# States' products by column halves, a softmax in token halves, and a new order of all steps, in an attention and SoLU feed-forward kernel

## The chip, the cores and the metric

The kernel runs on one core of one Trainium2 chip. The metric is the device time of one execution in microseconds. PE is the tensor engine, DVE the vector engine, ACT the scalar engine, POOL the engine GpSimd, SP the engine that issues the transfers.

## The reference: what is computed

Eight batch entries b with eight heads each hold 512 tokens x and 32 states. Tokens read the states, and states read the tokens, each with a softmax; the results, concatenated by heads, are 4608 rows of 512 (per entry 512 tokens and 32 states). Each row goes through a feed-forward layer with a softmax-gated activation and a layer norm.

```python
scores = scale * np.matmul(x, state.transpose(0, 1, 3, 2));  a = softmax(scores)   # +1e-9 in the sum
xread = np.matmul(a, state)
scores2 = scale * np.matmul(state, x.transpose(0, 1, 3, 2)); a2 = softmax(scores2)
sread = np.matmul(a2, x)
x = concat([xread, sread], axis=2)            # as 4608 rows of 512
h = x @ w_in                                  # 512 -> 1024
solu = h * softmax(h)
ln = (solu - mean(solu)) / np.sqrt(var(solu) + 1e-06) * g_ln
out = ln @ w_out                              # 1024 -> 512
```

The host lays the inputs out; w_in and w_out arrive as 64-bit words, of which the kernel makes float32.

## The kernel before

For a token, `xread @ w_in` equals `a @ (state @ w_in)`, summed over heads. So the kernel first makes, for each entry, the product of its states with w_in (step V, a matrix of 256 x 1024, in two blocks j of 128 rows), and H is then the attention weights times that matrix. State reads go the direct way, through w_in itself.

All work is written as small generators, one per step, each with `yield` between its instructions. The names of steps, as they stand in ORDER and in the prediction:

- `l n`: load of a block of w_in (n = 0 to 7: four row chunks c, left and right half of the columns; even n are the left halves) or of w_out (n = 8 to 15). `cl n`, `c n`: making float32 of it, a rounding on ACT (tile r) and three steps on DVE or POOL (tile wf). `wi c`, `wg f`, `wo n`: splits of w_in into a high and a low part (whi, wlo), scaling of w_out by g (wog), and its split (wohi, wolo).
- `Ls`, `G`: load of the states and their copies (s2). `LT`, `Ln`: loads of x, transposed and plain. `Lg`: four small loads of g.
- `V b i`: products of the states of entry b with column half i of w_in, and their copies out of PSUM (tiles swps, then vt or swf). `Y`, `Z`: V of entries 2 to 7 goes to memory and comes back later. `P`: its split into high and low part (swh, swl).
- `S b`: scores. `E b`: softmax over tokens, for the states' reads, and a bounce through memory (e2T, e2b). `A b`: softmax over states, for the tokens (a, m, z, aT), and its split (ath, atl). `R b`: reads of the states (srps).
- `H t`, t = 0 to 33: the 128 x 1024 tile h of token tile t. `C t`: its chain, a maximum (sm), an exponential (e), a product (u), centring, squares, and the inverse root. `D t`: transpose of u on DVE (ub), out to memory (ut) and back in another layout (back). `T t`: its split into uh and ul. `O t`: output products, the scaling (osb), and the store.
- `K`: one product of the identity with itself into a bank that nobody reads, a warming product.

Entry 0 uses the float32 matrices as they are (two products per half of an H step), the other entries and output tiles from 2 on use three products of high and low parts.

PSUM is split into two tiles h of two banks each (pool ps_h) and four single banks (pool ps_t), which scores, V, R and O share. SBUF's large blocks come from one pool of 45 slots; the column of per-tile numbers, sm, has four slots.

The order is written out by hand: the string ORDER names the step that is to go on next, and each token issues the instructions up to the next `yield` (`K*48` is 48 of them). Every engine runs its own instructions in this order and waits where an operand isn't ready, so one that waits holds up everything behind it on its engine. A second table, OPT, says for each step which engine takes it (a for ACT, d for DVE, p for POOL). All transfers are issued by SP, in order, and each waits until the eighth one before it has landed.

Of the kernel before, what the change touches and what calls it, by code (L numbers as in the profile page):

```python
# [28 lines left out]
OPT = dict(ph=2, k4=45, direct=[0, 1], hn=[0], on=[0, 1], s2='dpad', add='dpppdpdpdppppppp', whi='aada',  # L29
           wlo='ddpp', wg='aaaaaada', woh='aaaa', wol='dddd', ev='aaaaaaaadaaaaaaaaaadaaadaaaadddd',  # L30
           swh='aaaaaddadadadaaa', swl='ppdpddpppdddddpp', sub='dddpppdd', mul='ppddpdpp', ath='aaaaadda',
           alo='ddddddpp', up='aaaaaaaaadddaddadaddaadaadaaaaddda',
           uh='aaaaaddaaaddaaaaaaddddaadddddddaaaaaddaaaadddaadadaddaaadaaaddaaaaad',
           ul='ppppdppppppppdppddppppdddppppppdddddppddppppdddpdppppppddpdppdpdddpp',
           oe='aaaaaddaaddddadaadadadaddaaddddaaa')
# [3 lines left out]
E0 A0 c1 LT21 cl3 A0 E0 wi0 E0 l5 l6 G2 Lg A0 E0 cl4 A0 Ln01 G2 A0 c2 Ln10 c2 c3 c2 A0 K*48 S1 Ln11 A0 l7 c4 A0 c4  # L39
l8 cl5 l9 c5*2 A0 l10 c5 c4 E0 cl6 c3 l11 c6 c3 c6 l12 wi1 c6 l13 E1 A1 E1*2 l14 c7*2 cl7 K*50 V00 E1 l15 cl8 c7 c8  # L40
V00*2 Ln20 E1 c8 E1 K*6 V01 c8 LT30 cl9 E1*2 wg0 V01 c9*2 V01 K*7 H0 E1 A1 cl10 c9 A1 V10 cl11 LT31 A1 wg1 R0 Ln21
V10 R0 c10*2 V10 H0 R0 cl12 Ln30 c10 c11 A1 V11 Ln31 c12 wg2 c12 R0 wo4 C0 H1 c12 V11 R0*2 A1 V11 V20 C0 A1 H1 V20
A1 P10 C0 E1 V20 V21 C1 C0 H2 c13 V21 D0 V21 Y20 V30 C0 Y21 c14*2 D0 H2 c13 V30 C0 c11 V30 A1 P11 V31 c11 C1 C2 V40
wo4 V31 V40 R1 Y30 C1 V40 R1 P11 V31 V41 R1 C1 P10 Y31 V50 V41 H3 V50 Y40 V41 D0 V50 c15 Y41 C1 c15 V51 Z20 wi0 C2
C1 V60 D1 H3 V51 V60 Y50 V51 D1 V60 C2 V61 Y51 A1 C3 V70 V61*2 Y60 H4 A1 H4 T0 Y61 V71 T0 V70 P20 V70 H4 O0 V71 C2
V71 O0 Y70 wi1 D1 C2 O0 Y71 Z21 D2 H4 wg3 Z30 C2 H4*2 C3 wi2 D2 O0 R1 wg4 C3 wi2 S2 cl13 R1*2 O0 cl14 Z31 E2 C3 A2
H5 c14 H5 A2 H5 C3 A2 H5 c13 H5 T1 H5 A2 T1 O1 C3 cl15 O1 wo5 D3 E2 O1 c15 E2 wo5 O1 D3 A2 O1 D2 wg5 wg6 E2 wg7 O0
A2 E2 wi3 O0 A2 D3 O0 E2 A2 wi3 O1 wo6 E2 O1 O0 O1 T2 O0 C4 wo7 O2*2 T2 O2 O1 T2 O2 T3 T2 C4 C5 O2 O1 O3*2 wo7 C5
T3 O3*2 O2 C4 O2*2 C5 H6 C4 H6*2 T3 D4 H6 C5 H6 T3 H6 D4 O3 C5 O3 D5 O3*2 C4 C5 wo6 H7 D5 H7*2 C4 P21 O3 P21 O3*3
D4 O2 O3 O2 D5 O2 C6 O2 H7 O2 H7 Z40 P20 Z41 H7 T4 O2 S3 LT40 E2 C6 T4 O4 E3 E2 O4 T4 T5 O4 E3 C6 E3 T5 O5*3 E3 C6  # L50
T4 O5 T5 O5 C6 O5 O3 O4 E3 D6 T5 O5 E3 O5 C7 O5 D6 C6 O5*2 E3 E2 C7 O5 E3 O4*2 O5 E3 O4*2 A2 D6 O4*2 C7 A2 O4*2 P30
R2 C7 A2 R2 LT41 O4 E3 H8*2 R2 D7 C7 O4 R2 H8*2 R2 C7 R2 D7 A3 H8 T6 H8 A3 H9 T6 A3 H9 S4 C8 T6 A3 H9*2 E4 C8 H9 T6
# [20 lines left out]
H25*2 T22 O20 C24 O22 A7 O22*2 O20 C24 O22 A7 O20 O22*2 C25 C24 H26*2 A7 H26 C24 O21 H26*2 D24 H26 T23 C24 O22 C25
O23 A7 D24 O23 T23 A7 O23 T23 O23*3 O22*2 C25 T23 O23*2 C25 O23*2 D25 O23 C25 D24 O23 H27 O23 D25 C25 H27 P71 E7
H27*2 T24 P70 H27 A7 E7 O24*2 T24 O24 D25 A7 O24 H27 P71 O22 T24 O24 E7 O24 O22*2 R6 O22 A7 C26 R6 T25 O22 O24 O25
C27 C26 O25*2 R6 O25 T24 C27 C26 R7 O23 R7 C27 T25 C26 H28*2 C26 H28 D26 H28*2 C27 T25 C26 H28 D26 H29*2 C27 D27
T25 H29*3 D27 C27 H29 D26 O25*5 D27 O25*3 O24 O25 O24*2 C28 O24*2 T26 R6 C28 O24 T26 O26*2 R7 O24 C29 R7 T27 O26
# [552 lines left out]
```

## Time and profile before

| what | us |
|---|---|
| median of 3 runs | 384.27 (383.28 to 384.5) |
| profiled execution, device time | 384.67 |
| its span | 382.6 |
| PE busy | 370.2, of it 34.5 warming products |
| DVE busy | 316.1 |
| ACT busy | 204.8 |
| POOL busy | 170.0 |
| mean granted clock of PE | 0.997 |

Busy times are of the profiled execution. A row of the timeline gives the start in us from the span's start, the duration, engine, line, operation, output and inputs, and a count of instructions; in square brackets stand the idle time ahead of it and who ended that. A row of groups gives the busy time in us and the mean of one in ns, then idle time ahead and its causes. A row of stages gives, for each stretch, the busy time of each engine, the granted clock of PE, the busy share of the DMA engines and GB/s. Fp32 products leave two records each. Matmuls overlap, so the time of one on PE is read from the starts of those that follow.

### The profile page before, as it was taken

Reading aid. Unit: us, or ns where it says so; the run is one execution under the profiler, and the core shown is the slowest. Engines: PE = TensorE matmul, PEld = TensorE weight load, DVE = VectorE, ACT = ScalarE, POOL = GpSimd, SP = SyncE. Lnnn points to the kernel's source line nnn. Section 1 sums busy time; section 2 is a strip of 40 time slices with the busy share of each in tenths; the row PEclk is TensorE's granted clock in tenths of the full one; section 3 lists DMA queues with packets and bytes.
Section 4 is the critical chain, followed back from the end, with each engine's and each line's share of the span. In section 5 each row is a group of like instructions: output and inputs, shape, how many; then the busy total and the mean of one; then the engine's idle time right before and its main releaser. Section 6 shows DMA issues by size and latency. Waiting matters only on the chain.

```text
span 382.6 us, 6649 instructions
## 1 busy us (share of the span) xinstructions
PE 370.2 (97%) x2482; PEld 275.5 (72%) x2482; DVE 316.1 (83%) x421; ACT 204.8 (54%) x328; POOL 170.0 (44%) x229
## 2 busy tenths in 40 slices
PE   8999998999999999998999999999999999999994
PEld 8878433354677688775678887886878787888884
DVE  0899999979979999998998899898999928748420
ACT  1525797979656684526325266672673639234510
POOL 1144245157466345864245423645517835324220
PEclk9999999999999999999999999999999999999998
DMA  7999995997179928869966649359644662444431
GB/s 260 338 395 396 403 354 232 356 400 272 61 229 338 349 90 284 334 188 276 373 242 210 204 151 316 138 189 339 230 146 178 209 220 114 161 164 137 167 138 55
DMA packets 47051, 92.18 MB, mean 241 GB/s; under 512 B 4140, under 2 KB 25900, under 8 KB 47020
## 3 DMA queue, kind: packets, MB, share of 16 engines
q1 hardware_dynamic: 47020, 91.77, 68.0%
q8 instruction: 19, 0.31, 0.3%
q14 instruction: 12, 0.10, 0.1%
HBM read 54.53 MB, written 37.22 MB: 240 GB/s over the span
## 4 chain that ended last, share of the span: by engine, by line
PE 41%; DVE 29%; DMA 20%; issue 4%; ACT 3%; SPq 1%; POOL 0%; DVEq 0%; ACTq 0%; POOLq 0%
PE o L525 24%; PE h L451 14%; DVE ub L488 3%; DVE sm L458 3%; DVE u L464 3%; DMA st<-stB_dram 3%; DMA raw<-w_out_dram 3%; DMA back<-ut 3%; DVE ul L134 3%; DMA raw<-w_in_dram 3%; DMA xn<-xn_dram 2%; DMA ut<-ub 2%; DMA kept<-vt 2%; DMA xT<-xT_dram 2%; DVE uh L131 1%
## 5 line engine op out<-in xcount | busy, mean ns | idle before, releaser
L134 POOL TENSOR_TENSOR ul<-back,uh 128x512 fp32r<-128x512 f32 x39 | 52.1, 1341 | 50.1 <-DVE uh L131 26.8
L525 PE MATMUL o<-wohi,uh 128*128 128x512 f32 (+1 forms) x264 | 70.3, 388 | 1.2 <-DVE osb L534 0.9
L525 PE MATMUL o<-wolo,uh 128*128 128x512 f32 (+1 forms) x264 | 70.0, 385 | 0.0
L525 PE MATMUL o<-wohi,ul 128*128 128x512 f32 (+1 forms) x264 | 69.1, 384 | 0.4 <-DVE ul L134 0.4
L461 ACT ACTIVATE e<-h,sm 128x1024 f32<-128x1024 f32 x34 | 37.9, 1116 | 52.8 <-DVE sm L458 47.8
L525 PEld LDWEIGHTS o<-wohi,uh 128*128 128x128 f32 x264 | 48.2, 188 | 13.4 <-issue 3.1
L525 PEld LDWEIGHTS o<-wohi,ul 128*128 128x128 f32 x264 | 48.6, 188 | 11.4 <-DVE ul L134 1.1
L525 PEld LDWEIGHTS o<-wolo,uh 128*128 128x128 f32 x264 | 48.5, 188 | 9.8
L458 DVE TENSOR_REDUCE sm<-h 128x1 f32<-128x1024 f32 x34 | 41.2, 1212 | 15.0 <-ACT osb L532 12.0
L476 ACT ACTIVATE e<-u 128x1024 f32<-128x1024 f32 x34 | 36.0, 1059 | 26.7 <-DVE u L471 26.1
L464 DVE SCALAR_TENSOR_TENSOR u<-h,e 128x1024 f32<-128x1024 f32 x34 | 41.1, 1213 | 6.8 <-ACT e L461 6.8
L488 DVE STREAM_TRANSPOSE ub<-u 128x1024 f32<-128x1024 f32 x34 | 41.9, 1236 | 4.3 <-ACT u L469 3.0
L480 POOL TENSOR_TENSOR sm<-sm 128x1 f32<-128x1 f32 x34 | 8.8, 260 | 63.6 <-ACT e L476 62.7
L451 PE MATMUL h<-swh,ath 128*128 128x512 f32 x112 | 36.2, 407 | 0.9 <-DVE u L464 0.9
L549 PEld LDWEIGHTS warm<-ident 128*128 128x128 f32 x282 | 33.5, 200 | 4.7 <-issue 3.4
L549 PE MATMUL warm<-ident 128*128 128x128 f32 x282 | 34.5, 286 | 1.3 <-POOL ident masks.py:199 1.3
L451 PE MATMUL h<-swh,atl 128*128 128x512 f32 x112 | 35.0, 394 | 0.0
L451 PE MATMUL h<-swl,ath 128*128 128x512 f32 x112 | 34.7, 391 | 0.0
L129 ACT ACTIVATE uh<-back 128x512 fp32r<-128x512 f32 (+1 forms) x40 | 24.1, 621 | 12.3 <-DMA back<-ut 12.3
L469 ACT ACTIVATE u<-u,sm 128x1024 f32<-128x1024 f32 x21 | 24.1, 1148 | 8.7 <-DVE u L464 8.5
L532 ACT ACTIVATE osb<-o,sm 128x512 f32<-128x512 f32 (+1 forms) x19 | 12.4, 660 | 28.8 <-PE o L525 28.6
L451 PEld LDWEIGHTS h<-swh,ath 128*128 128x128 f32 x112 | 20.1, 188 | 9.4 <-issue 3.6
(88 smaller groups left out, 577.6 us busy)
## 6 DMA issues: line engine op xcount, KB each, us to landing
ut<-ub SPq DMA_DIRECT2D x34, 512.0 KB, 3.3
...
```

The costliest lines, as they stand in the source:

```text
L129: nc.scalar.activation(out, src, AF.Copy)
L134: engine(k).tensor_tensor(out=out, in0=a, in1=hi.bitcast(F32), op=ALU.subtract)
L451: nc.tensor.matmul(ph[t][:, cols], left[l][:, p, tok], right[r][:, cols], start=(p, l, r) == (0, 0, 0), stop=(p, l, r) == (parts - 1, *kin ...
L458: nc.vector.tensor_reduce(nm, ph[t], AX.X, ALU.max, negate=True)
L461: nc.scalar.activation(e, ph[t], AF.Exp, bias=nm, accum_out=z)
L464: nc.vector.scalar_tensor_tensor(out=u, in0=ph[t], scalar=1.0, in1=e, op0=ALU.mult, op1=ALU.mult, accum_out=su)
L469: nc.scalar.activation(u, u, AF.Identity, bias=su, scale=-float(DF))
L476: nc.scalar.activation(e, u, AF.Square, scale=float(DF) ** -0.5, accum_out=ss)
L488: nc.vector.transpose(ub, us[t][0])
L525: nc.tensor.matmul(po, ut[t][l][:, f, :], w[NP + f // 2][:, f % 2, cols], start=(hf, l, w is wohi, q) == (0, 0, True, 0), stop=(hf, l, q) ...
L532: nc.scalar.activation(o[:, cols], po, AF.Copy, scale=us[t][1])
L549: nc.tensor.matmul(warm, ident, ident, start=True, stop=True)
```

## The change

Four things change.

1. V of entries 0 and 1 goes into a tile of the pool ps_h, one half of the columns of both blocks j into its two banks, instead of two banks of ps_t.
2. `softmax_states` takes a part: for entry 0 it runs twice, for tokens 0 to 255 and 256 to 511 (steps Ah00 and Ah01), with tiles half as wide; the tiles of H take the half in which their tokens lie.
3. The four loads of g are four yields of `Lg`, where they were one.
4. ORDER and the engines in OPT are new throughout. The left halves of w_in (l0, l2, l4, l6) are loaded and converted first, and V00, V10, V20 and V30, which need them alone, stand ahead of every score.

```diff
-OPT = dict(ph=2, k4=45, direct=[0, 1], hn=[0], on=[0, 1], s2='dpad', add='dpppdpdpdppppppp', whi='aada',
+OPT = dict(ph=2, k4=45, direct=[0, 1], hn=[0], vh=[0, 1], ah=[0], on=[0, 1], s2='pppp', add='dpdpdpdpddpddddp',
...
-K Ls0 LT00 LT01 l0 l1 l2 l3 G0 Ls2 G0 Lg K*29 S0 l4 Ln00 E0 cl0 LT10 c0 E0 c0 E0 LT11 c0 cl1 E0 c1 cl2 LT20 E0 c1
+K l0 l2 Ls0 l4 Lg l6 l1 l3 c0 cl0 LT00 c0*2 cl2 LT01 c2*3 G0 Ls2 c4 cl4 l5 G0 c4 l7 cl6 l8 c4 c6 cl1 Lg c6*2 c1 cl3
...
@@ load_g
-        yield
+            yield
@@ state_w_in
-        ps = [bank([HALF], f"swps{b}_{j}_{n}") for j in range(NJ)]
+        if b in OPT["vh"]:
+            both = ps_h.tile([P, DF], F32, tag="h", name=f"swph{b}_{n}")
+            ps = [both[:, j * HALF:(j + 1) * HALF] for j in range(NJ)]
+        else:
+            ps = [bank([HALF], f"swps{b}_{j}_{n}") for j in range(NJ)]
@@ softmax_states
-    def softmax_states(b):
-        a = block([NJ * S], F32, f"a{b}")
+    def softmax_states(b, part=0, parts=1):
+        width = S // parts
+        a = block([NJ * width], F32, f"a{b}_{part}")
         for j in range(NJ):
-            nc.vector.transpose(a[:, j * S:(j + 1) * S], scores[b][j])
+            nc.vector.transpose(a[:, j * width:(j + 1) * width], scores[b][j][:, part * width:(part + 1) * width])
             yield
...
-            res[b] = [aT]
+            res.setdefault(b, []).append(aT)
@@ h_steps
+                if b in OPT["ah"]:
+                    left = [res[b][t % NT // 2]]
+                    tok = slice(t % 2 * P, (t % 2 + 1) * P)
@@ steps
+        if b in OPT["ah"]:
+            for part in range(2):
+                step(f"Ah{b}{part}", softmax_states, b, part, 2)
+        else:
+            step(f"A{b}", softmax_states, b)
```

PE, the start of the program, before: warming products, the scores of entries 0 and 1 (sps), and V00 (swps0), the first of the states' products.

```order
L549 MATMUL warm_83<-ident_71 128x128 x30
L186 MATMUL sps0_0_137<-xT0_0_87,s2_0_99 32x512 x4
L186 MATMUL sps0_1_138<-xT0_1_89,s2_0_99 32x512 x4
L549 MATMUL warm_83<-ident_71 128x128 x48
L186 MATMUL sps1_0_266<-xT1_0_155,s2_0_99 32x512 x4
L186 MATMUL sps1_1_267<-xT1_1_163,s2_0_99 32x512 x4
L549 MATMUL warm_83<-ident_71 128x128 x50
L186 MATMUL swps0_0_0_383<-wf0_157,s2_0_99 32x512 x2
```

The same place now; swph are the tiles in ps_h, and V20 and V30 (swps2, swps3) are in single banks.

```order
L559 MATMUL warm_83<-ident_71 128x128 x61
L188 MATMUL swph0_0_209<-wf0_100,s2_0_116 32x512 x2
...
L188 MATMUL swph1_0_222<-wf0_100,s2_0_116 32x512 x2
...
L188 MATMUL swps2_0_0_239<-wf0_100,s2_0_116 32x512 x2
...
L559 MATMUL warm_83<-ident_71 128x128 x5
L188 MATMUL swps3_0_0_265<-wf0_100,s2_0_116 32x512 x2
...
L559 MATMUL warm_83<-ident_71 128x128 x5
L188 MATMUL sps0_0_293<-xT0_0_104,s2_0_116 32x512 x4
```

Four groups of products now stand where two scores stood, and fewer warming products in all: 91, where there were 141.

DVE, its first instructions before: the maximum of entry 0's scores (sc0) and the first conversions of w_in (wf0).

```order
L131 COPY s2_0_99<-st0_85 64x512
L332 TENSOR_REDUCE sc0_151<-sps0_0_137 128x1
L230 TENSOR_SCALAR wf0_157<-raw0_91 128x512
L233 SCALAR_TENSOR_TENSOR wf0_157<-raw0_91,wf0_157 128x512
L236 ISA wf0_157<-wf0_157,r0_153 128x1024
L332 TENSOR_REDUCE sc0_151<-sps0_1_138 128x1
L230 TENSOR_SCALAR wf0_157<-raw1_93 128x512
```

And now: from the last left half (raw6) to the first half-wide softmax.

```order
L232 TENSOR_SCALAR wf3_135<-raw6_94 128x512
L235 SCALAR_TENSOR_TENSOR wf3_135<-raw6_94,wf3_135 128x512
L238 ISA wf3_135<-wf3_135,r6_130 128x1024
L232 TENSOR_SCALAR wf0_100<-raw1_96 128x512
L232 TENSOR_SCALAR wf1_112<-raw3_98 128x512
...
L235 SCALAR_TENSOR_TENSOR wf3_135<-raw7_128,wf3_135 128x512
L366 STREAM_TRANSPOSE a0_0_312<-sps0_0_293 128x256
```

All eight blocks of w_in are converted ahead of the first softmax step, the four left ones (with their last step on DVE) first.

ACT, around the last scalings of w_out (wog7), on which the last two products of O0 depend, before:

```order
L129 ACTIVATE uh1_961<-back1_879 128x512 x2
L219 ACTIVATE r15_973<-raw15_394 128x512
L129 ACTIVATE wohi5_976<-wog5_540 128x1024
L338 ACTIVATE e2T2_983,sc2_939<-sps2_0_920,sc2_939 128x512
L368 ACTIVATE a2_942<-a2_942 128x1024
L254 ACTIVATE wog6_914<-wf6_538,ngT_79 128x512
L254 ACTIVATE wog7_995<-wf7_627,ngT_79 128x512
```

And now:

```order
L131 ACTIVATE uh0_729<-back0_626 128x512 x2
L256 ACTIVATE wog5_742<-wf5_492,ngT_79 128x512 x2
L256 ACTIVATE wog6_754<-wf6_546,ngT_79 128x512 x2
L375 ACTIVATE a1_0_724<-a1_0_724 128x1024
L256 ACTIVATE wog7_766<-wf7_560,ngT_79 128x512
L471 ACTIVATE e2_770,sm2_601<-h2_523,sm2_601 128x1024
L221 ACTIVATE r15_776<-raw15_415 128x512
L131 ACTIVATE swh1_0_778<-swf1_0_220 128x1024
L471 ACTIVATE e3_785,sm3_749<-h3_691,sm3_749 128x1024
L256 ACTIVATE wog7_766<-wf7_560,ngT_79 128x512
```

The last scalings now stand behind the exponential of entry 1's softmax (a1), where it was that of entry 2, and in between O0's split (uh0) and theirs stand fewer steps.

More of the change, by code (lines that the diff above doesn't have):

```diff
@@ L27 @@
 NTILES = B * NT + B * NS // P
-OPT = dict(ph=2, k4=45, direct=[0, 1], hn=[0], on=[0, 1], s2='dpad', add='dpppdpdpdppppppp', whi='aada',
[L30 to L35, printed above, removed]
@@ L37 @@
-ORDER = """
-K Ls0 LT00 LT01 l0 l1 l2 l3 G0 Ls2 G0 Lg K*29 S0 l4 Ln00 E0 cl0 LT10 c0 E0 c0 E0 LT11 c0 cl1 E0 c1 cl2 LT20 E0 c1
[L39 to L52, printed above, removed]
@@ L73 @@
[L73 to L77, printed above, removed]
@@ L83 @@
-C33 O31*3 C33 O31*3 C33 O31*2 C33 D33 O31 O30*2 O31 C33 D33 O30 T32 O30*2 T32 O30*2 T32 O30 T32 O30 D33 O30*2 O32
-O30 O32*2 O30 O32*4 T33 O32 O31 T33 O32*4 T33*2 O33 O32 O33*4 O32 O33*23
+OPT = dict(ph=2, k4=45, direct=[0, 1], hn=[0], vh=[0, 1], ah=[0], on=[0, 1], s2='pppp', add='dpdpdpdpddpddddp',
+           whi='aaaa', wlo='dddp', wg='aaaaaaaa', woh='aaaa', wol='dpdp', ev='aaaaaaaaaaaaaaaaaaaaaaaaaaaaaaaa',
+           swh='aaadaadadaadddad', swl='pppppdpdpdddppdd', sub='dpddpddp', subh='dpdd', mulh='dpdd', mul='pddddpdd',
+           ath='aaddaddd', alo='dddpddpd', up='aaadaadaaaddddaaaaadddddaaddaddadd',
+           uh='aadaaaaaaaadaaddaaaaadaadaaadddddadddaaddddaaddadaaaaaaddddaddaadadd',
+           ul='ppppdpdpppdppdpddpdppddpddpddddppdddpdpddppppdppdddddpppppdpppddppdp',
+           oe='aaaaaaaddaaaaaaaaaadadddadaaaddada')
@@ new lines @@
+ORDER = """
+K l0 l2 Ls0 l4 Lg l6 l1 l3 c0 cl0 LT00 c0*2 cl2 LT01 c2*3 G0 Ls2 c4 cl4 l5 G0 c4 l7 cl6 l8 c4 c6 cl1 Lg c6*2 c1 cl3
+Ln00 K*60 V00 c3*2 V10 c1 Ln01 V00 c3 V00 V20 V10 Ln10 V10 c1 V20 l9 V20 K*5 V30 G2 wi0 c5 l10 G2 c5 V30 l11 V30
+K*5 S0 c7 cl5 c7 l12 cl7 c5 Ah00 Lg Ah00 cl8 Ah00 l13 wi1 Ah00 c7 E0 Ah00 l14 c8 wi2 K*15 V01 E0 Ah00 LT10 Ah00 E0
+V11 Ah00*2 V01 LT11 Ah01 V01 Ah01 K*3 V40 Ah01 V11 LT20 c9 V11 Ah01 H0 c9 V40 l15 V40 Ah01 E0 V50 Lg cl9 c8 E0 H0
+c8 E0 Ah01 V50 Ah01 V50 c9 V60 Ah01 cl10 C0 H1 cl11 Ah01 V60 E0 V60 E0 V21 C0 H1 c10 E0 c10 V21 C0 c10 V21 Y20 V70
@@ new lines @@
+H25 T21 D23 H24 A7 O21 T21 O21 E6 O21 D22 O21 T21 A7 E6 O21*2 D23 O21 P71 E6 O21*2 A7 T21 O21 E7 H24 A7 H24 T22 O21
+E7 C24 O21 E7 T22 O22*2 O21 C24 O22 T22 O22 O21 T22 O22 C24 O22*2 E6 O22 T23 C24 A7 O22 T23 A7 O23 O22 C24 O22 D24
+O22 T23 C24 O23*2 A7 D24 H26 T23 R6 A7 R6 Ln71 H26*2 R6 C25 H26 D24 R6 H26 O22 C25 H26 R6 O23 R6 O22 E7 O23 C25 E7
+O23 E7 O23*2 C26 C25 H27*2 T24 H27 C25 D25 H27*2 C26 C25 A7 H27 D25 O23*2 P71 O23*2 O24 T24 O24 C26 D25 T24 O24*2
+C26 O24 H28 D26 C26 O24*2 T24 O24 D26 C26 O24 O23 O24 E7 T25 O24 O23 E7 O24 O25 O24 T25 O25 E7 O25 P70 D26 T25 O25
@@ L369, in softmax_states @@
         yield
-        z = sbuf("z1", shape, F32, f"z1_{b}")
+        z = sbuf("z1", shape, F32, f"z1_{b}_{part}")
         nc.vector.tensor_reduce(z, seg, AX.X, ALU.add)
@@ L375, in softmax_states @@
         yield
-        engine(of("mul", b)).tensor_tensor(out=seg, in0=seg, in1=z.broadcast_to(seg.shape), op=ALU.mult)
+        engine(of("mul", b) if parts == 1 else of("mulh", 2 * b + part)).tensor_tensor(out=seg, in0=seg, in1=z.broadcast_to(seg.shape), op=ALU.mult)
         yield
-        aT = block([NJ, S], F32, f"aT{b}")
+        aT = block([NJ, width], F32, f"aT{b}_{part}")
         nc.vector.transpose(aT.rearrange("p j s -> p (j s)"), a)
         if b in OPT["hn"]:
-            res[b] = [aT]
+            res.setdefault(b, []).append(aT)
         yield
```

71 lines of the change are left out of this document (42 added, 29 removed).

## The prediction

> **What bounds the kernel now.** I read the page's first part, the tensor engine's timeline from its start, then the engines' busy time by stages. The profiled execution took 384.67 us, 382.6 of them its span; the median of the runs is 384.27. What the change saves of the profiled execution is taken from 384.27.
>
> ```profile
> PE 370.2 (97%) x2482; PEld 275.5 (72%) x2482; DVE 316.1 (83%) x421; ACT 204.8 (54%) x328; POOL 170.0 (44%) x229
> L549 PE MATMUL warm<-ident 128*128 128x128 f32 x282 | 34.5, 286 | 1.3 <-POOL ident masks.py:199 1.3
> ```
>
> ```profile
> 1.34 8.65 PE L549 MATMUL warm<-ident 128*128 128x128 f32 x60 [1.34 <-POOL ident masks.py:199]
> 24.08 11.43 PE L549 MATMUL warm<-ident 128*128 128x128 f32 x100
> 35.44 1.15 PE L186 MATMUL swps<-wf,s 64*32 64x512 f32 x16
> 40.74 1.88 PE L451 MATMUL h<-swf,aT 128*128 128x512 f32 x4
> 42.55 1.09 PE L186 MATMUL swps<-wf,s 64*32 64x512 f32 x16
> 43.57 1.10 PE L403 MATMUL srps<-xn,e 128*32 128x64 f32 x64
> 75.79 2.74 PE L519 MATMUL o<-wog,uh 128*128 128x512 f32 x6
> 79.75 1.02 PE L519 MATMUL o<-wog,uh 128*128 128x512 f32 x2
> 80.70 0.45 PE L414 MATMUL srT<-ident,sr 128*64 128x64 f32 x8
> 103.12 2.88 PE h L451 x12
> 279.76 1.07 PE L525 MATMUL o<-wohi,uh 128*128 128x512 f32 x4
> ```
>
> Columns: start, duration, line, output and inputs, count (an fp32 product leaves two records). The 97% hides 34.5 us of warming products, which compute nothing; but for two scores, PE does no work before 35.44. From there it is nearly dense.
>
> ```profile
> core 0: us, PE busy (x) PEld busy (x) DVE busy (x) ACT busy (x) POOL busy (x), PEclk, DMA share, GB/s
> 0.00:20.00 20.00, 18.66 (x157) 17.70 (x158) 9.09 (x16) 7.52 (x12) 3.34 (x11) 1.00 0.91 302
> 20.00:72.00 52.00, 50.79 (x552) 27.25 (x558) 50.96 (x72) 34.50 (x57) 21.61 (x23) 1.00 0.93 351
> 72.00:280.00 208.00, 203.93 (x1210) 150.88 (x1195) 193.35 (x255) 116.74 (x187) 105.38 (x138) 1.00 0.72 250
> 280.00:361.00 81.00, 80.09 (x481) 64.98 (x480) 59.29 (x77) 41.30 (x64) 36.37 (x53) 1.00 0.49 168
> ```
>
> DVE is 98% busy from 20 to 72 us (50.96 of 52), 93% from 72 to 280. So PE bounds the kernel by its late start, and DVE almost as closely behind that. A gain on PE counts as far as DVE can follow.
>
> **The change: PE's opening.** The new order holds 91 warming products for 141. Fifty took 11.43 us at 24.08, 0.229 each: 11.4 us less. I walk the new order. The first 61 take 8.65 for thirty, then 31 x 0.229 = 7.1, from 1.34 on: V00 at 17.1. A group of states' products takes 1.02 (42.55 to 43.57), half an H step of entry 0 takes 1.88, a read's 64 products about 1.03. After V00, V10, V20, 5 warming products, V30 and 5 more stands S0, at 23.5 to 24.5; fifteen warming products later V01, at 28.0; V40 at 30.7; H0 at 31.7, where it stood at 40.74.
>
> Are the data there?
>
> ```profile
> 4.89 0.42 DVE L131 COPY s<-st 64x512 f32<-64x512 f32 x1 [4.89 <-DMA st<-stB_dram]
> 9.95 0.69 ACT L219 ACTIVATE r<-raw 128x512 uint32<-128x512 uint32 x1 [7.95 <-DMA raw<-w_in_dram]
> 11.65 0.42 DVE L230 TENSOR_SCALAR wf<-raw 128x512 uint32<-128x512 uint32 x1
> 12.11 0.69 DVE L233 SCALAR_TENSOR_TENSOR wf<-raw,wf 128x512 uint32<-128x512 uint32 x1
> 12.95 0.69 DVE L236 CUSTOM_DVE_ANT_0 wf<-wf,r 128x1024 uint16<-128x1024 uint16 x1
> 15.45 1.28 POOL L236 TENSOR_TENSOR wf<-wf,r 128x512 uint32<-128x512 uint32 x1 [0.81 <-ACT e2T L338]
> ```
>
> The first load was used at 4.89, the fourth at 9.95: 1.69 each; 512 KB at the 351 GB/s of 20 to 72 is 1.49. The left half of w_in's last chunk (l6) is now fifth behind the first of the large loads: 12.3 to 13.3, then a rounding (0.7) and three DVE steps (1.7): ready by 15.7, ahead of 17.1. For V01 the thirteenth large load, l7, lands at 22.8 to 25.2; with a rounding, two DVE steps (1.1) and POOL's addition (1.28) it is ready at 25.9 to 28.3, for 28.0. Cost: 0, at most 0.3.
>
> **To the end of O0.** PE's work ahead of O0 is sixteen V and two scores (18.4), eight halves of H (15.0), a read and its transposes (1.4): densely, O0 starts at 59. Its last two products need w_out's last columns. ACT scales these behind the exponential of entry 1, which waits for S1, DVE and POOL.
>
> ```profile
> L368 ACT ACTIVATE a<-a 128x1024 f32<-128x1024 f32 x8 | 8.4, 1054 | 5.4 <-POOL a L366 3.0 <-DVE a L366 2.4
> L366 POOL TENSOR_TENSOR a<-a,m 128x1024 f32<-128x1024 f32 x3 | 6.1, 2045 | 4.8 <-DVE m L364 4.8
> L364 DVE TENSOR_REDUCE m<-a 128x32 f32<-128x1024 f32 x8 | 9.7, 1209 | 0.1
> L461 ACT ACTIVATE e<-h,sm 128x1024 f32<-128x1024 f32 x34 | 37.9, 1116 | 52.8 <-DVE sm L458 47.8 <-DMA kept<-vt 2.3 <-issue 1.9
> L254 ACT ACTIVATE wog<-wf,ngT 128x512 f32<-128x512 f32 x7 | 4.9, 716 | 2.4 <-POOL wf L236 2.3
> ```
>
> S1 ends half an H step ahead of O0, at 57.4. I summed DVE's new rows from S0 on with each wait for PE and ACT: the transpose of tile 1's u ends at 58.1, a W_in difference (1.1) and entry 1's two transposes (0.6 each) at 60.5, its maximum (1.2) at 61.7; POOL's subtraction (2.05) at 63.8, ACT's exponential (1.05) at 64.8. Behind that stand a scaling (0.7), an exponential (1.1), a rounding (0.7), a swh (1.0), an exponential (1.1) and the last scaling (0.7): 70.1. O0's last product ends at 70.8 or later, not 66.8. This stall gives back 4.0 us (0 if that chain runs ahead of my walk, 6 if DVE is late). PE then has 42.3 us of work done. Before, it had as much done at 80.70: all V, S0, S1, eight halves of H, two reads, O0's first four products at 0.94, H4's twelve at 0.23 (2.88 at 103.12). **PE's lead: 9.9 us**, from the 11.4, some 2.5 us of waits that go, and the 4.0.
>
> **DVE's lead is smaller.** At 69.3 it has 54.2 us of its rows behind it (start-to-start times, in issue order). Before, it was as far at 72.45: **3.1 us**. The earlier start brings DVE less, because before it worked while PE warmed: its rows issued ahead of H0 sum to 25.9 us in the old order and 17.9 in the new.
>
> ```profile
> 72.45 1.22 DVE L134 TENSOR_TENSOR atl<-aT,ath 128x1024 fp32r<-128x1024 f32 x1
> 281.04 1.22 DVE L366 TENSOR_TENSOR a<-a,m 128x1024 f32<-128x1024 f32 x1
> ```
>
> The programs meet at O22's first product (279.76 before): 1185 products of PE stand ahead of it in both, and 318 instructions of DVE in the old one, 319 in the new, in both 245.5 us by those start-to-start times. DVE stood at this place at 281.04. With DVE as idle as before, O22 comes 3.1 us earlier; with PE's losses as before, 9.9. Reaching 281.04 - 9.9 from 69.3 takes DVE 96% busy; it was 98% busy from 20 to 72. I take the middle, a gain of **6.3** (94%): of DVE's 15 idle us in that stretch those shrink in which it waited for PE, not those in which it waited for ACT or a transfer, and no row says how many these are.
>
> **Work that changes engines.** Ahead of O22 it cancels on DVE, by that sum. Behind it DVE has 83 instructions for 69.
>
> ```profile
> L134 DVE TENSOR_TENSOR ul<-back,uh 128x512 fp32r<-128x512 f32 x25 | 20.0, 804 | 3.2 <-ACT uh L129 3.1
> L471 DVE TENSOR_SCALAR u<-u,sm 128x1024 f32<-128x1024 f32 x13 | 10.7, 823 | 0.3
> L131 DVE CAST uh<-back 128x512 fp32r<-128x512 f32 x28 | 18.6, 668 | 2.1 <-DMA back<-ut 2.1
> L134 DVE TENSOR_TENSOR swl<-swf,swh 128x1024 fp32r<-128x1024 f32 x8 | 9.7, 1215 | 0.1
> ```
>
> Two more u (1.6), four uh (2.7), an ul (0.8), two swl (2.4) and pieces of softmax: 9.6 us, of which 8.4 ahead of the last transpose of u. They lie in DVE's idle 21.7 us of 280 to 361 (81 less 59.29): cost 0, and 8.4 without that cover. POOL loses 14 us of work and ACT 2; neither bounds anything. SP's queue has the same 197 transfers. Entry 0's half-wide steps are not in the trace; by the 1024-wide ones they cost half to all of 1.2 us each, and the walk takes half.
>
> A row on POOL and DVE together:
>
> ```profile
> 180.89 2.38 POOL L134 TENSOR_TENSOR swl<-swf,swh 128x1024 fp32r<-128x1024 f32 x1
> 181.12 2.71 DVE L134 TENSOR_TENSOR ul<-back,uh 128x512 fp32r<-128x512 f32 x1
> ```
>
> The ul took 2.71 for a mean of 0.80, and lasted as long as POOL's swl. The Trainium skill (SBUF — State Buffer, Who interferes with whom) says that a DVE instruction with two SBUF inputs contends with POOL's reads and that the first to issue keeps the shared ports for its whole length; this row agrees. As an estimate by that rule, DVE's five additional ul ahead of O22, one of them so held, would make the gain 1.9 smaller.
>
> Sum: 6.3 + 0 = 6.3 us: **378.0 us**.
>
> **The rivals.** *Nothing is given back* (14%): DVE runs at 98%, 193.35/0.98 = 197 us from 69.3, so it is at O22's place at 266.6 for 281.04, 14 us earlier: 370. For it: PE now has slack to feed DVE. Against: DVE's 15 idle us of 72 to 280, and PE would have to lose less there too. *The lead goes on the way* (15%): DVE idles as before (3.1 left), and late loads and a late S1 take 2 more: 382 to 385.4, typically 383.2. For it: 93% is what 208 us of trace show. *Slower* (16%): DVE becomes the bound behind O22.
>
> ```profile
> DVE sm L458 <- ACT osb L532: 12.0, 5, 6.3
> 314.76 1.23 DVE L458 TENSOR_REDUCE sm<-h 128x1 f32<-128x1024 f32 x1 [6.30 <-ACT osb L532]
> 360.73 1.25 DVE L488 STREAM_TRANSPOSE ub<-u 128x1024 f32<-128x1024 f32 x1 [1.22 <-ACT u L469]
> ```
>
> A tile's maximum waits until an output four tiles earlier has been scaled, since sm has four slots; so DVE can't run ahead, and its idle time there need not shrink. If all 21.7 us recur, the last transpose (360.73 before, 22 us ahead of the end) comes 8.4 - 6.3 us later: 386.4. It decides once more than 19.6 of the 21.7 recur. Against it: PE is 99% busy there (80.09 of 81), so these waits end when PE's work ends.
>
> **How the numbers follow.** The forecast (55%) has 374 to 382, by a gain of 9.9 at one end and the 3.1 less one late load at the other. A measurement tells 0.3%, 1.15 us, from no change: 383.1 to 385.4. Faster: 55 + 14 and a fourth of the second rival, 73%; same 10%; slower 17%. The range leaves out half of the best case and the worse half of the slow one: 371 to 387.
>
> **What would show it.** In the changed kernel's trace: 182 records of warming products and V00 near 17, H0 near 32 (right: the opening); a wait of O0 for the scaled w_out near 66 to 70; DVE's transposes at entry 1 near 60; O22's first product near 273 with DVE 94% busy from 70 on; no wait above 3 us on PE behind it. Wrong: V00 past 19 (loads), O22 past 277 (DVE no better fed), or the last transpose of u past 360 (tail).

## The result and the profile after

| | before | changed |
|---|---|---|
| median of the runs, us | 384.38 (383.28 to 385.29) | 378.18 (377.3 to 378.99) |
| ratio, 95% interval | | 0.9839 (0.9805 to 0.9874) |
| profiled execution, its span | 384.67, 382.6 | 377.94, 375.6 |
| O22's first product | 279.76 | 270.70 |
| from there to the end of the span | 102.8 | 104.9 |
| mean granted clock of PE | 0.997 | 0.990 |

The change is 6.2 us faster, where 6.3 were forecast. The two places the prediction named did not move by what it said, though: O22 came 9.1 us earlier, not 6.3, and what follows it took 2.1 us longer, not the same.

Of the changed kernel, the profile's busy times and the warming products:

```profile
PE 360.5 (96%) x2382; PEld 266.7 (71%) x2382; DVE 316.7 (84%) x436; ACT 202.5 (54%) x332; POOL 156.3 (42%) x220
L559 PE MATMUL warm<-ident 128*128 128x128 f32 x182 | 24.4, 298 | 1.3 <-POOL ident masks.py:199 1.3
```

PE's timeline: V00, H0, O0 with its last product, H4, and O22's first product:

```profile
17.66 1.95 PE L188 MATMUL swph<-wf,s 64*32 64x512 f32 x32
...
32.56 1.98 PE L461 MATMUL h<-swf,aT 128*128 128x512 f32 x4
...
61.05 6.28 PE L529 MATMUL o<-wog,uh 128*128 128x512 f32 x14 [0.42 <-ACT uh L131]
70.07 1.12 PE L529 MATMUL o<-wog,uh 128*128 128x512 f32 x2 [2.74 <-ACT wog L256]
73.41 2.33 PE L461 MATMUL h<-swh,ath 128*128 128x512 f32 x4 [2.22 <-DVE u L474]
...
270.70 1.07 PE L535 MATMUL o<-wohi,uh 128*128 128x512 f32 x4
```

The opening is as walked: V00 at 17.7, H0 at 32.6. O0 starts at 61.05 and its last product waits 2.74 us for the scaled w_out. Then comes a wait the prediction did not have, 2.22 us of H4 for DVE's u. The rows of DVE and POOL at that place show what is late:

```profile
69.34 2.79 DVE L133 CAST swh<-swf 128x1024 fp32r<-128x1024 f32 x1
72.04 1.21 DVE L474 SCALAR_TENSOR_TENSOR u<-h,e 128x1024 f32<-128x1024 f32 x1
...
279.32 0.69 DVE L133 CAST ath<-aT 128x1024 fp32r<-128x1024 f32 x1
69.22 2.35 POOL L136 TENSOR_TENSOR swl<-swf,swh 128x1024 fp32r<-128x1024 f32 x1
```

H4 needs the PSUM of tile 2, which is free once u has read it. Ahead of u, DVE copies entry 1's second swh; that copy took 2.79 us, beside POOL's swl of 2.35; a copy of the same shape, at 279.32, took 0.69. And in the second of these two waits the clock column falls (stages of 4 us; the figure behind POOL's is the granted clock):

```profile
70.00:74.00 4.00, 1.72 (x4) 0.80 (x4) 4.00 (x4) 1.66 (x3) 3.31 (x2) 0.68 1.04 408
74.00:78.00 4.00, 4.00 (x10) 2.80 (x9) 3.96 (x6) 4.00 (x8) 3.45 (x7) 0.50 0.94 365
78.00:82.00 4.00, 4.00 (x29) 2.31 (x29) 2.83 (x4) 4.00 (x6) 3.15 (x4) 0.96 0.88 258
```

From about 71.5, half a us into the second wait, to 78.3 PE runs at half clock, and the sixteen products of H4 and H5 up to the next scores take 6.26 us (73.41 to 79.67).

A stretch of about equal work on PE up to O22, first of the kernel before, then of the changed one (the first still holds three products of O0, 2.8 us; the second a read, the scores of entry 2 and two products of H, 2.9 us):

```profile
83.00:280.00 197.00, 193.18 (x1126) 146.14 (x1125) 185.12 (x246) 108.43 (x174) 102.28 (x135) 1.00 0.70 242
```

```profile
78.00:271.00 193.00, 191.87 (x1209) 147.08 (x1209) 185.35 (x246) 106.86 (x175) 95.25 (x128) 1.00 0.74 251
273.00:354.00 81.00, 78.77 (x472) 63.12 (x471) 60.02 (x81) 35.38 (x57) 27.60 (x49) 1.00 0.48 165
```

The third row is of the changed kernel behind O22. DVE was busy for 185 us in 197 and in 193 us; PE stood 3.8 us before and 1.1 now. Two of the waits of before that are gone, on its timeline of PE:

```profile
176.60 1.06 PE L186 MATMUL sps<-xT,s 64*32 64x512 f32 x8 [1.29 <-DMA xT<-xT_dram]
184.63 1.17 PE L525 MATMUL o<-wohi,uh 128*128 128x512 f32 x4 [0.92 <-DVE osb L534]
```

Behind O22 PE stands 2.2 us in 273 to 354, where it stood 0.9 in 280 to 361; that is 1.3 of the 2.1 us, and the rest is not traced. Three waits of PE and, ahead of them, one of DVE:

```profile
287.31 0.43 DVE L133 CAST uh<-back 128x512 fp32r<-128x512 f32 x1 [2.17 <-DMA back<-ut]
291.79 0.73 PE L535 MATMUL o<-wohi,ul 128*128 128x512 f32 x2 [0.96 <-DVE ul L136]
293.02 0.70 PE L461 MATMUL h<-swh,ath 128*128 128x512 f32 x2 [0.50 <-DVE u L474]
304.53 1.20 PE L535 MATMUL o<-wohi,uh 128*128 128x512 f32 x4 [0.77 <-ACT uh L131]
```

So the account of O22's 9.1 us: a lead of 9.7 at the end of O0 (80.70 before, 71.0 now, 0.94 behind the start of its last product), less 2.2 (the wait for u), less 2.4 (the slow products: 6.26 for the 3.9 they take at full clock, below), plus 4 (the stretch of 197 in 193: 2.7 of it are waits of PE, 1.3 busy time).

### The profile page after: what moved, and what is told of

It reads as the page before. It is cut to its first block, busy times and chain, and to the rows that moved or that the text cites. A ratio compares the mean times of both kernels' runs of the same rounds, so it can differ in the third digit from the quotient of the medians.

```text
span 375.6 us, 6452 instructions
## 1 busy us (share of the span) xinstructions
PE 360.5 (96%) x2382; PEld 266.7 (71%) x2382; DVE 316.7 (84%) x436; ACT 202.5 (54%) x332; POOL 156.3 (42%) x220
## 4 chain that ended last, share of the span: by engine, by line
PE 65%; DVE 17%; issue 6%; DMA 6%; ACT 3%; POOL 1%; SPq 0%; DVEq 0%; POOLq 0%
PE o L535 32%; PE h L461 20%; PE warm L559 6%; DMA back<-ut 5%; DVE u L474 3%; PE swps L188 2%; DVE ub L498 2%; DVE ul L136 2%; PE sps L188 2%; DVE sm L468 1%; DMA ut<-ub 1%; DVE a L383 1%; PE swph L188 1%; DVE z L378 1%; PE srps L410 1%
## 5 line engine op out<-in xcount | busy, mean ns | idle before, releaser
L535 PE MATMUL o<-wohi,ul 128*128 128x512 f32 (+1 forms) x264 | 71.5, 385 | 1.0 <-DVE ul L136 1.0
L535 PE MATMUL o<-wolo,uh 128*128 128x512 f32 (+1 forms) x264 | 70.9, 384 | 0.0
L136 POOL TENSOR_TENSOR ul<-back,uh 128x512 fp32r<-128x512 f32 x33 | 45.4, 1382 | 55.8 <-ACT uh L131 30.7
L468 DVE TENSOR_REDUCE sm<-h 128x1 f32<-128x1024 f32 x34 | 41.3, 1214 | 17.1 <-ACT osb L542 12.4
L542 ACT ACTIVATE osb<-o,sm 128x512 f32<-128x512 f32 (+1 forms) x25 | 16.6, 664 | 37.2 <-PE o L535 32.9
L461 PE MATMUL h<-swl,ath 128*128 128x512 f32 x112 | 35.9, 406 | 0.0
L490 POOL TENSOR_TENSOR sm<-sm 128x1 f32<-128x1 f32 x34 | 9.7, 285 | 57.8 <-ACT e L486 57.3
L461 PEld LDWEIGHTS h<-swh,ath 128*128 128x128 f32 x112 | 21.2, 194 | 10.5 <-issue 5.9
L479 ACT ACTIVATE u<-u,sm 128x1024 f32<-128x1024 f32 x17 | 19.5, 1149 | 13.5 <-DVE u L474 13.3
L559 PEld LDWEIGHTS warm<-ident 128*128 128x128 f32 x182 | 23.3, 211 | 4.8 <-issue 3.4
L461 PEld LDWEIGHTS h<-swl,ath 128*128 128x128 f32 x112 | 20.9, 193 | 7.2 <-issue 1.7
```

The lines of the kernel that those rows point to most:

```text
L136: engine(k).tensor_tensor(out=out, in0=a, in1=hi.bitcast(F32), op=ALU.subtract)
L461: nc.tensor.matmul(ph[t][:, cols], left[l][:, p, tok], right[r][:, cols], start=(p, l, r) == (0, 0, 0), stop=(p, l, r) == (parts - 1, *kin ...
L468: nc.vector.tensor_reduce(nm, ph[t], AX.X, ALU.max, negate=True)
L479: nc.scalar.activation(u, u, AF.Identity, bias=su, scale=-float(DF))
L535: nc.tensor.matmul(po, ut[t][l][:, f, :], w[NP + f // 2][:, f % 2, cols], start=(hf, l, w is wohi, q) == (0, 0, True, 0), stop=(hf, l, q) ...
L559: nc.tensor.matmul(warm, ident, ident, start=True, stop=True)
```

## The experiments

Theory: PE's start, and what holds PE at 67 to 79 us, set O22's place; DVE follows though it is 96% busy. Rival: DVE sets the pace from 70 us on, and PE's lead counts in part, as the forecast's mean supposed. All edits are to the changed kernel; the ratio is to the kernel before. The last three columns are of the profiled execution, in us.

| run | median | ratio (95%) | H0 at | H4/H5's end to O22 | O22 to the end |
|---|---|---|---|---|---|
| changed kernel | 378.18 | 0.9839 (0.9805, 0.9874) | 32.56 | 191.0 | 104.9 |
| e4_late | 383.79 | 0.9993 (0.9969, 1.0017) | 38.84 | 192.4 | 102.6 |
| e5_whole | 380.24 | 0.9901 (0.9866, 0.9935) | 34.26 | 192.7 | 104.7 |
| e12_banks | 381.79 | 0.9929 (0.9908, 0.9950) | 35.31 | 192.9 | 105.4 |
| e8_dve | 380.21 | 0.9908 (0.9884, 0.9933) | 32.60 | 194.2 | 103.8 |
| e1_wog | 377.72 | 0.9826 (0.9788, 0.9863) | 31.80 | 191.2 | 103.6 |
| e2_swh | 374.10 | 0.9738 (0.9717, 0.9758) | 31.61 | 191.3 | 104.9 |
| e3_both | 375.57 | 0.9768 (0.9735, 0.9801) | 32.16 | 192.1 | 105.1 |
| e7_warm | 374.32 | 0.9758 (0.9736, 0.9781) | 32.03 | 190.0 | 102.3 |
| e10_fill | 373.12 | 0.9721 (0.9688, 0.9755) | 31.98 | 190.6 | 102.5 |
| e6_tail | 376.57 | 0.9806 (0.9780, 0.9832) | 31.90 | 190.9 | 103.4 |
| e9_xn | 379.17 | 0.9868 (0.9833, 0.9904) | 32.50 | 192.0 | 103.8 |
| e11_all | 371.64 | 0.9684 (0.9657, 0.9710) | 30.66 | 190.8 | 102.4 |

H0 stands between 31.6 and 32.6 where the opening is untouched, so one execution differs from the next by up to a us there.

**A later start.**

```diff
-Ln00 K*60 V00
+Ln00 K*90 V00
```

> The changed kernel with 30 more warming products ahead of the first states' product, 30 x 0.229 = 6.9 us: PE's opening is late by that, DVE's work ahead of it is not. Theory of the prediction: PE's start and DVE decide together, so about half of the delay reaches the end: 381 to 382.5, O22's first product at 273.5 to 275. Rival: PE's start alone decides the gain; all 6.9 come back, 385. Second rival: the start does not matter, the gain comes from other places of the new order: 378 to 379.

Measured: 383.79, 5.6 us more. PE's timeline of this run, H0 and O22:

```profile
38.84 1.98 PE L461 MATMUL h<-swf,aT 128*128 128x512 f32 x4
...
278.24 1.20 PE L535 MATMUL o<-wohi,uh 128*128 128x512 f32 x4 [0.93 <-ACT uh L131]
```

Thirty products are 6.9 us. The delay is 6.28 us at H0, 7.54 at O22 (0.93 of it one wait) and 5.6 in the median; behind O22 this execution is 2.3 us shorter (102.6 for 104.9), with a short write there (below). DVE had all that time to work ahead, and at O22 it brought nothing. The rival of the start alone is right up to O22, and the forecast's half is wrong.

**Two parts of the change undone.** The softmax of entry 0 in one piece, and PSUM for V as before:

```diff
-ah=[0]
-K*5 S0 c7 cl5 c7 l12 cl7 c5 Ah00 Lg Ah00 cl8 Ah00 l13 wi1 Ah00 c7 E0 Ah00 l14 c8 wi2 K*15 V01 E0 Ah00 LT10 Ah00 E0
+ah=[]
+K*5 S0 c7 cl5 c7 l12 cl7 c5 A0 Lg A0 cl8 A0 l13 wi1 A0 c7 E0 A0 l14 c8 wi2 K*15 V01 E0 A0 LT10 A0 E0
...
```

> One part of the change undone in the new order: entry 0's softmax over states is done for all tokens at once, its steps at the places where those of the first half stood, its multiplication on DVE; H0 therefore waits for the whole. Theory: the halves bring H0 forward because a chain of seven steps of half the width stands ahead of it (about 0.6 us less in each, on DVE and ACT); without them H0 comes 3 to 4.5 us later than 32.56, and as the 6.3 us later start of the previous run came back to five sixths, 2.5 to 3.8 us of that reach the end: 380.5 to 382. Rival: H0 is not held by this chain, since w_in's halves and the products ahead of it set its place; the time stays at 378, or falls a little, since DVE has seven instructions fewer.

```diff
-vh=[0, 1]
+vh=[]
```

> One part of the change undone in the new order: the states' products of entries 0 and 1 take four single banks of PSUM again, as those of the other entries, and not the two double ones that stand empty until the first h. Theory: then four groups of products and the scores of entry 0 need ten single banks in 7 us where four exist, each freed by a copy on ACT of about 0.55; the third and fourth group and S0 wait for these, H0 comes 1.5 to 3 us later than 32.56, and five sixths of that reach the end: 379.5 to 380.8. Rival: the copies keep up, since ACT is free there; 378.

H0 and the wait ahead of it in the first, and the first wait of the products in the second:

```profile
34.26 1.95 PE L461 MATMUL h<-swf,aT 128*128 128x512 f32 x4 [1.82 <-ACT vt L131]
```

```profile
30.66 2.83 PE L188 MATMUL swps<-wf,s 64*32 64x512 f32 x24 [0.93 <-ACT swf L131]
```

H0's row in the first names ACT's copy of V, which ends at 34.25; entry 0's softmax on DVE ends at 34.12, so the two end nearly together. The halves are worth 1.7 us at H0 (less than the 3 to 4.5 expected) and 2.1 in the median, where the interval of the ratio overlaps the changed kernel's; the double banks 2.75 at H0 and 3.6 in the median, beyond the intervals. In the second the four left groups kept their places; it was V01 and V11 that waited for banks, not V20, V30 and S0. Of three delays of H0 (1.7, 2.75, 6.3) the end shows 2.1, 3.6 and 5.6: about all of each, within the us that executions differ by.

**DVE relieved.** Seven shifts of u and three scalings of outputs, of tiles 7 to 21, from DVE to ACT:

```diff
-up='aaadaadaaaddddaaaaadddddaaddaddadd'
+up='aaadaadaaaaaaaaaaaaaaaddaaddaddadd'
-oe='aaaaaaaddaaaaaaaaaadadddadaaaddada'
+oe='aaaaaaaaaaaaaaaaaaaaadddadaaaddada'
```

> The changed kernel with ten operations between 105 and 215 us taken from DVE to ACT: the shifts of u of seven tiles (0.8 us each) and the scalings of three outputs (0.7 each), 7.7 us of DVE's 193. Theory: in the changed kernel PE loses only 3 to 4 us between 80 and 270 us, and the lateness of O22 is set by PE's start and its two waits near 70; DVE, 96% busy, follows without delaying it, so the time stays within 1 us of 378.2. Rival: DVE sets O22's place, as the prediction's mean of the two leads supposed; then up to half of the 7.7 come out, 374.5 to 376. Second rival: ACT's queue, where they now stand, delays exponentials, and it becomes slower, 379 to 381.

The stretch 105 to 215, changed kernel first:

```profile
105.00:215.00 110.00, 108.90 (x717) 84.00 (x716) 106.25 (x148) 60.19 (x100) 48.31 (x69) 1.00 0.78 265
```

```profile
105.00:215.00 110.00, 107.45 (x709) 82.75 (x709) 99.69 (x137) 63.51 (x103) 47.01 (x68) 1.00 0.76 256
```

DVE fell from 97% to 91% busy, and the kernel became 2.0 us slower. So less load on DVE did not make PE faster. The time is the one of the second rival, by which ACT's longer queue delays its exponentials; it is not shown that this is the reason. Which of the ten moves makes PE lose 1.5 us more here is not settled: the longest wait is 1.34 us at 179.48 for a uh of DVE, while ACT is 58% busy.

**The two waits at 67 to 73 us.** The last scaling of w_out earlier:

```diff
-C3 O0 / Y70 wg4 ... O0 A1 O0 wg6 A1 C2 O0 A1*2 cl15 P10 c15 A1 D1 C3 P11 P10 Z21 C2 wg7 A1 O0
+C3 O0 cl15 / Y70 wg4 ... O0 A1 c15 O0 wg6 A1 C2 wg7 O0 A1*2 P10 A1 D1 C3 P11 P10 Z21 C2 A1 O0
```

> The changed kernel with one thing moved: the rounding of w_out's last chunk, its addition and its last scaling are issued earlier, ahead of ACT's exponential for tile 2. The changed kernel ran 378.2 us. Theory: O0's wait of 2.74 us at 70.07 is this last scaling; it falls under 0.7 us. But the next products, H4's, wait until DVE has read tile 2's and 3's h, at 72.0 to 73.4, and this is not moved: the wait only changes its place, H4's grows from 2.2 to about 5, and the time stays within 0.8 us of 378.2. Rival: the wait is on the path by itself; H4 comes 2.7 us earlier, 375.5.

Entry 1's second swh on ACT:

```diff
-swh='aaadaadadaadddad'
+swh='aaaaaadadaadddad'
```

> The changed kernel with one operation on another engine: the rounded copy of entry 1's second states' W_in (swh) goes from DVE, where it took 2.79 us at 69.34 beside POOL's subtraction, to ACT. Theory: tile 2's and 3's h are then read 2.8 us earlier, so H4 starts right behind O0, near 71.3 for 73.41; PE has one gap less, so the granted clock, 0.50 from 72 to 78, recovers earlier or does not fall, worth up to 2.4 us more. At O22's first product 2 to 4 us are left of it: 374 to 376. Rival: DVE decides from here to O22 (96% busy); it gets 2.79 less, so at most 2.8 come out, and the clock is worth nothing: 375.4 to 376.5 with the fall of the clock still there. Second rival: PE has room later and nothing comes out: 378.

And both:

> Both edits, the earlier last scaling of w_out and swh on ACT. Theory: neither wait at 67 to 73 us is left, H4 starts near 69.5, the clock stays at 1.00 and the ten products of H4 and H5 take 2.3 us for 4.7; O22's first product, at 270.7 in the changed kernel, comes 3 to 6 us earlier, 372 to 375. Rival: DVE is the bound from 70 to O22; then this is no faster than swh on ACT alone.

O0's last product and H4, in the three kernels in this order (of the third H4 alone; its O0 waits 0.52 as in the first):

```profile
66.85 1.12 PE L529 MATMUL o<-wog,uh 128*128 128x512 f32 x2 [0.52 <-ACT wog L256]
72.01 2.34 PE L461 MATMUL h<-swh,ath 128*128 128x512 f32 x4 [4.04 <-DVE u L474]
```

```profile
69.98 2.08 PE L529 MATMUL o<-wog,uh 128*128 128x512 f32 x2 [3.68 <-ACT wog L256]
71.06 2.36 PE L461 MATMUL h<-swh,ath 128*128 128x512 f32 x4
```

```profile
71.19 2.07 PE L461 MATMUL h<-swh,ath 128*128 128x512 f32 x4 [2.81 <-ACT ath L131]
```

With the scaling alone the wait only moves to H4, and the time is the same (377.7). With swh on ACT H4's wait is gone, and 4.1 us come out of the medians; counted from H0, O22 and the end of the profiled execution are 2.3 us earlier (O22 238.1 us behind H0, now 235.9), so 2.3 to 4.1 are the edit's. About half of it comes through the clock: counted from O0's start H4 comes 1.3 us earlier, and the sixteen products take 5.07 us (71.06 to 76.13) for 6.26, since the clock is back at 72.9, 1.8 us behind H4's start, where it was 4.9. With both, H4 waits for ath instead, which stands behind swh in ACT's queue: no better than swh alone. So the wait for w_out, which the prediction named, was not the binding one. What was binding is the copy that DVE makes beside POOL. That it is long because of POOL is read from its row; no run moves POOL's work away from it.

**The clock.** The waits of the changed kernel filled with warming products:

```diff
-C2 wg7 A1 O0 C3 C2 H4
+C2 wg7 A1 K*12 O0 C3 C2 K*9 H4
```

> The changed kernel with warming products inside PE's two waits at 67 to 73 us: 12 ahead of O0's last product, 9 ahead of H4 (12 x 0.229 = 2.75 and 9 x 0.229 = 2.06 us, as long as the waits of 2.74 and 2.22). PE waits for the same things and computes nothing more that is used. Theory: the granted clock falls to 0.50 from 72 to 78 us because PE stood still; kept busy it stays at 1.00, the ten products of H4 and H5 take 2.3 us for 4.7, and 1.5 to 2.4 us reach the end: 375.8 to 376.7. Rival: the clock does not follow from the standstill; it falls as before and the time is 378 or up to 0.5 more. Second rival: the clock holds, but DVE sets the pace from here to O22, and nothing comes out.

Stages of this kernel:

```profile
70.00:74.00 4.00, 3.77 (x26) 2.91 (x24) 4.00 (x5) 1.69 (x3) 3.37 (x2) 1.00 1.03 398
74.00:78.00 4.00, 3.43 (x14) 2.61 (x15) 4.00 (x5) 3.98 (x7) 3.53 (x5) 1.00 0.82 322
```

```profile
53.33 1.92 PE L188 MATMUL swps<-wf,s 64*32 64x512 f32 x24 [0.55 <-DVE sreadT L425]
56.04 1.06 PE L188 MATMUL swps<-wf,s 64*32 64x512 f32 x8 [0.79 <-ACT vt L131]
74.13 0.70 PE L461 MATMUL h<-swh,ath 128*128 128x512 f32 x2 [0.21 <-DVE u L474]
75.27 0.70 PE L461 MATMUL h<-swh,ath 128*128 128x512 f32 x2 [0.44 <-DVE u L474]
...
78.63 1.09 PE L188 MATMUL sps<-xT,s 64*32 64x512 f32 x16
```

The median is 3.9 us lower, by work without use. The clock stays at 1.00, and H4 and H5 take 4.50 us to the next scores (74.13 to 78.63), where they took 6.26. At the wait for u the next product starts 0.84 us behind the one before it, where the others start 0.23 apart, so 0.6 is lost there and 3.9 are left at full clock. The expectations count ten products here, and 2.3 us for them; the trace has sixteen. From O0's start to the scores of entry 2 it is 1.8 us less (16.84 for 18.62). The filling has a price of its own: by the code, the warming tile keeps one of the four single banks of PSUM to its last use, now 22 us later, and the products at 53 to 56 wait 1.3 us (0.55 and 0.79), which they did not before. Of the profiled execution, 4.0 us are gained from H0 on: 1.5 up to O22 (236.6 for 238.1), which is what the filling brings less its price, and 2.5 behind O22 (102.3 for 104.9), where the clock was 1.00 in both; these go with the short write there (below).

Both losses removed, swh on ACT and 16 warming products ahead of O0's last:

```diff
-swh='aaadaadadaadddad' ... C2 wg7 A1 O0 C3 C2 H4
+swh='aaaaaadadaadddad' ... C2 wg7 A1 K*16 O0 C3 C2 H4
```

> Entry 1's swh on ACT, and 16 warming products (16 x 0.229 = 3.7 us) ahead of O0's last product, whose wait there grew to 3.68. Theory: two different losses are removed, the late reading of h (DVE beside POOL) and the fall of the clock; H4 starts near 71 as with swh on ACT alone, and the clock, 0.64 from 70 to 74 there, stays at 1.00, so that H4's and H5's ten products end 1.3 to 1.8 us earlier; of this 1 to 2 us reach the end: 372.2 to 373.2. Rival: both edits remove the same loss, and the time stays at 374.1; what the first alone brought was then the clock.

373.1, by its interval not different from swh alone (374.1). From H0 to O22 it takes 236.4 us, 0.6 more than with swh alone: sixteen were too many, O0's last product started at 71.59 for 69.98, and H5 then waited 1.12 us for atl. What the clock would bring on top of swh on ACT is therefore not measured; the fall there was already short (3.4 us).

**Behind O22.** The copy that stood at 287 on ACT, and a load moved off from between the writing and the reading back of tile 24:

```diff
-uh='aadaaaaaaaadaaddaaaaadaadaaadddddadddaaddddaaddadaaaaaaddddaddaadadd'
+uh='aadaaaaaaaadaaddaaaaadaadaaadddddadddaaddddaaddaaaaaaaaddddaddaadadd'
```

> The changed kernel with one operation moved behind O22: the rounded copy of the first half of tile 24's returned block goes from DVE, where it held the queue 2.17 us at 285 to 287 until the block had landed, to ACT. Theory: behind O22 the changed kernel takes 2.1 us longer than the one before (104.9 for 102.8), because DVE's queue stands at this copy and PE then waits 0.96 us for ul at 291.8 and 0.50 for u at 293.0; without the stand both waits go, 1.0 to 1.5 us: 376.7 to 377.2. Rival: ACT now stands there instead, its squares and exponentials come later and PE waits as long: 378 or more.

```diff
-R6 Ln71 H26*2 R6 C25 H26 D24 R6 H26
+R6 H26*2 R6 C25 H26 D24 Ln71 R6 H26
```

> The changed kernel with one transfer moved on SP's queue: entry 7's load of xn (its second half), which stood between the writing of tile 24's block and its reading back, is issued behind the reading. In the changed kernel the write was issued at 278.12 and the reading, which waits for it, at 282.74, 4.6 us later; with warming products in the waits near 70 it was 2.9, and there PE had no wait above 0.3 us behind O22. Theory: the load's traffic holds the write up; without it the reading is issued about 1.7 us earlier, DVE's wait of 2.17 us shrinks under 0.6, PE's waits of 0.96, 0.50 and 0.77 go mostly, and what follows O22's first product falls from 104.9 to 102.5 to 103.3: 376.0 to 376.8. Rival: the write is late by chance of the memory, not by this load; nothing changes: 378.

SP's queue, changed kernel, then the one with the load moved, then the one with filled waits:

```profile
278.12 0.32 SPq L316 DMA_DIRECT2D ut<-ub  x1
278.53 0.39 SPq L199 DMA_DIRECT2D xn<-xn_dram  x1
282.74 0.37 SPq L321 DMA_DIRECT2D back<-ut  x1
```

```profile
278.92 0.32 SPq L316 DMA_DIRECT2D ut<-ub  x1
283.60 0.37 SPq L321 DMA_DIRECT2D back<-ut  x1
```

```profile
276.07 0.32 SPq L316 DMA_DIRECT2D ut<-ub  x1
...
278.95 0.37 SPq L321 DMA_DIRECT2D back<-ut  x1
```

The theory of the load falls: with it out of the way the write still took 4.7 us. But the length of this write does go with the length of the tail: in nine kernels it was 3.9 to 4.9 us from issue to the reading, and O22 to the end took 103.4 to 105.4; in the four others (a later start, filled waits, both losses removed, and all together) 2.7 to 2.9, and 102.3 to 102.6. What makes it long or short is not settled: the load stood behind the write in three of the four, and not in the kernel with the load moved, where it was long. The copy on ACT took away DVE's stand and the 0.96 us wait, not the long write; 1.6 us come out of the medians, but its interval overlaps the changed kernel's, so that this is likely, not shown.

**Together,** with seven warming products fewer at the start:

```diff
-Ln00 K*60 V00
+Ln00 K*53 V00
```

and the edits of swh, of the 16 products and of the load:

> Swh on ACT, 16 warming products ahead of O0's last product, entry 7's xn load behind the reading of tile 24, and seven warming products fewer ahead of the first states' product (53 for 60, 1.6 us; the left half of the last chunk of w_in was ready near 13.6 for products at 17.66). Theory: the four losses are apart and add up, the start by five sixths: 1.3 for the start, 1 to 2 for the transfer where a wait is left, so 1.3 to 3 below the same without the last two edits: 370 to 372. Rival: the first product of the right halves (28.61) is held by their load and POOL's addition, which ended near 27.1, so that the earlier start ends in a wait there; then no more than 0.5 for it, 372 to 373.

PE's timeline: V00, V01 and H0:

```profile
15.76 1.95 PE L188 MATMUL swph<-wf,s 64*32 64x512 f32 x32
...
26.70 1.95 PE L188 MATMUL swph<-wf,s 64*32 64x512 f32 x32
...
30.66 1.98 PE L461 MATMUL h<-swf,aT 128*128 128x512 f32 x4
```

371.64: 12.6 us less than before, 6.5 less than the changed kernel, faster than both beyond their intervals. Against the run with both losses removed H0 is 1.3 us earlier and the median 1.5 less, with intervals that overlap; V01 starts without a wait at 26.70, so its load does not hold it there.

## Why the prediction was right, step by step

**The opening: right.** 182 records, V00 at 17.66 (17.1 forecast), H0 at 32.56 (31.7). The loads were in time, as costed at 0.

**The end of O0: right in sum.** It ended at 71.0 for 70.8, by a start 2 us later than walked and a wait of 2.74 for a stall of 4.0. PE's lead: 9.7 for 9.9.

**What comes behind O0: missing.** The walk took H4 to follow O0. It waited 2.22 for u. The prediction had such a hold of DVE beside POOL's swl in a row, and cited the rule of the Trainium skill (SBUF — State Buffer, Who interferes with whom), but priced it on ul ahead of O22, as an estimate of 1.9, and passed over that the section counts a cast in a two-port mode among the operations that can be held; here it is such a copy, that of swh, 2.79 for the 0.69 of a rounded copy of the same shape later, and moving it is worth 2.3 to 4.1, about half of it through the clock. And the prediction gave PE a standstill of 4.0 us without asking what the clock does after one. The Trainium skill (TensorE: Matmul & The Clock Gate, What's actually happening) has the clock halved after some 3.4 us without work. With swh on ACT the trace comes near that: the clock fell 3.2 us into a wait of 3.68 (0.74 in the stage of 69 to 70). In the changed kernel it took less, half a us of a second wait behind one of 2.74 and a product of 1.1; the measurement decides. That was worth 2.4 us on the path.

**The middle, 6.3: mis-sized.** The step that failed is "Reaching 281.04 - 9.9 from 69.3 takes DVE 96% busy" with "I take the middle, a gain of 6.3 (94%)" (the middle of 3.1 and 9.9 is 6.5). It took PE's and DVE's leads as two ends between which O22 lies. The runs show PE's lead and not DVE's: 6.28 us of later start were 7.5 at O22, and 6.6 us less work for DVE from 105 to 215 brought no gain. From 72 to 273 DVE was 96% busy, the share that the prediction had for PE's full lead:

```profile
72.00:273.00 201.00, 198.46 (x1227) 152.03 (x1228) 193.28 (x258) 112.77 (x184) 100.65 (x134) 0.98 0.74 255
```

O22 gained 9.06. It is not that nothing was given back: 4.6 us were lost at 71 to 79 (2.2 and 2.4), and 4 won back, 2.7 of them since PE's waits of before did not recur.

**Behind O22, 0: mis-sized.** It cost 2.1. The work that moved to DVE did hide (60.02 us of 81, as 59.29 before; the last transpose of u at 355.39), as forecast, and no wait of PE is above 1 us; what the cost goes with is the write of tile 24's block, read back 4.6 us after its issue where four kernels have 2.7 to 2.9. No run shortened that write by itself, so that this is the cause is likely, not shown.

The gain at O22 was forecast too small by 2.8, and the cost behind it too small by 2.1: the two nearly cancel. That the time came out within 0.2 us is luck; the opening and the end of O0 are not.

**The rivals.** "Nothing is given back" needed DVE at 98%; it was at 96%. "The lead goes on the way" needed DVE to idle as before; it idled 7.7 us in the stretch of the tables above, where it idled 11.9. "DVE becomes the bound behind O22" fell with DVE 74% busy there.
